# Decode attention, two blocks of 32 heads: the last quad's PV is run from the loop's own code on TensorE

## Chip, cores, metric

The kernel runs on one core of a Trainium2 chip. The metric is the device time of one execution in microseconds (us). Three executions of the kernel before took 669.31, 669.55 and 671.23 us, a median of 669.55.

## What is computed

Two independent attention blocks, A and B, each for one new token: a query projection, attention of 32 heads over a cache of 8192 keys and values of 128 elements, and an output projection. The two outputs of 512 elements are put side by side. All inputs are bf16.

```python
def _A_ref(x, k_cache, v_cache, wq, wo):          # _B_ref is the same, rep = 1
    B, Sq, D = x.shape                            # 1, 1, 512
    H, Dh = 32, 128
    q = (x @ wq).reshape(B, Sq, H, Dh).transpose(0, 2, 1, 3)
    scores = jnp.einsum("bhqd,bhkd->bhqk", q, k_cache) * (Dh ** -0.5)
    p = _softmax(scores, axis=-1)
    o = jnp.einsum("bhqk,bhkd->bhqd", p, v_cache)
    return o.transpose(0, 2, 1, 3).reshape(B, Sq, H * Dh) @ wo
```

K and V of both blocks are 268 MB, the weights 17 MB; each byte is read once.

## The kernel before

**Tiling.** The 64 heads are taken as 16 quads, `n` = 0 to 15, four heads each; quads 0 to 7 belong to A, 8 to 15 to B. A quad's K is one load of 8.4 MB: head h sits on partitions 32h to 32h + 31, and each partition holds T = 256 keys of 128 elements. K has two buffers (`kn`, slots 0 and 1, quad n in slot n % 2); V has one (`vn`).

**One quad.** DVE multiplies K by the query in place in four chunks of 64 keys (`plan_mul`, line 331). PE adds up each product over the head's elements by 16 matmuls with the identity (`plan_red`, line 340), and DVE finishes that (`plan_sr`, line 351). DVE, PE and ACT find the maximum and the exponentials `pt` (`plan_max`, `plan_gmax`, `plan_exp`). `plan_sum` (line 393) adds up the denominators on PE. `plan_pv` (line 409) is PV: 256 matmuls, one for each key column t, with `vn[:, t, :]` as weights and the four columns `pt[:, t, :]` moving, all added up in `acc`. `plan_o` (line 419) scales the result into `oD`.

**Order.** Every engine has its own list of operations, made once in Python by `op` and `wait` and written out in that order. In turn n come the three first chunks' score work of quad n, then sum and PV of quad n - 1, then the last chunk of quad n, its maximum and exponentials. SP issues all large loads: K of quad n + 1 at the start of turn n, when the reductions of quad n - 1 are done; V of quad n at the end of turn n, when PV of quad n - 1 is done. In turn 15 the output weights of A (`load_wo(0, 0)`, 4 MB) and the first two groups of B's stand in the place of the next K.

**PE's loop.** On PE alone turns 1 to 15 are a hardware loop (`_emit_loop`): the body is written once, the semaphore values waited for are kept in registers that grow from round to round, and each reduction is there twice, for the two slots of K, with a compare-and-branch that picks one. Everything before and behind the loop is straight code.

**The end.** V of quad 15 is loaded in three parts, of 128, 64 and 64 key columns (`VLAST = (0, 128, 192, 256)`). Behind them SP issues B's groups 2 to 6 of output weights. B's output weights come in groups of heads `WOG[1] = [(0, 8), (8, 4), (12, 4), (16, 8), (24, 4), (28, 2), (30, 2)]`; A's are one group. `plan_relayout(a, g)` (lines 444 to 451: DVE, PE, DVE) brings a group's outputs into the layout that `plan_wo(a, g)` (line 461) wants: four matmuls of one column for each head, 128 for A. `early` is the list of B's groups 0 to 4, whose heads belong to quads before the last; groups 5 and 6 are the last quad's. Behind the loop PE's list is (lines 525 to 543): six re-layouts, wo(0,0), wo(1,0) and wo(1,1), the sum and PV of quad 15 in three parts, wo(1,2) to wo(1,4), re-layouts 5 and 6, wo(1,5), wo(1,6), and the output.

Of the kernel before, what the change touches and what calls it, by code (L numbers as in the profile page):

```python
# [14 lines left out]
class _Ctr:  # L15


    def __init__(self, nc, stack, name):
        self.sem = stack.enter_context(nc.semaphore(name))
        self.n = 0  # L20
        self.name = name
# [29 lines left out]
def _emit(e, items, slot=None):  # L51
    for fn, ctr, k in items:
        if fn is None:
            e.wait_ge(ctr.sem, k)
        elif isinstance(fn, tuple):
            which, fns = fn
            if slot is None:
                fns[which](e).then_inc(ctr.sem, k)
            else:
                with e.If_eq(slot, 0):  # L60
                    fns[0](e).then_inc(ctr.sem, k)
                with e.Else():
                    fns[1](e).then_inc(ctr.sem, k)
        elif ctr is None:
            fn(e)
        else:
            fn(e).then_inc(ctr.sem, k)


def _steps(items):  # L70


    out, waits = [], []
    for it in items:
        if it[0] is None:
            waits.append(it[1:])
        else:
            out.append((waits, it))
            waits = []
    assert not waits  # L80
    return out


def _emit_loop(e, rounds, slot):


    rounds = [_steps(r) for r in rounds]
    assert len({len(r) for r in rounds}) == 1
    early, body = [], []
    for k in range(len(rounds[0])):  # L90
        at = [r[k] for r in rounds]
        assert all(it[1:] == at[0][1][1:] for _, it in at)
        first, second, third = at[0][0], at[1][0], at[2][0]
        waits = []
        for (ctr, v), (_, w) in zip(second, third):
            d = w - v
            assert v - d >= 1
            waits.append((ctr, v - d, d))
        for n, (ws, _) in enumerate(at[1:], 1):
            assert [(c, v) for c, v in ws] == [(c, v + n * d) for c, v, d in waits]  # L100
        for ctr, v in first:
            same = [x for c, x, _ in waits if c is ctr]
            if not same:
                early.append((None, ctr, v))
            else:
                assert v <= same[0]
        body.append((waits, at[0][1]))
    _emit(e, early)
    regs = {}
    for k, (waits, _) in enumerate(body):  # L110
        for i, (ctr, v, d) in enumerate(waits):
            if d:
                regs[k, i] = e.alloc_register("w%d_%d" % (k, i))
                e.reg_mov(regs[k, i], v)
    sreg = e.alloc_register("slot")
    e.reg_mov(sreg, slot)
    with e.Fori(0, len(rounds)):
        for k, (waits, it) in enumerate(body):
            for i, (ctr, v, d) in enumerate(waits):
                e.wait_ge(ctr.sem, regs.get((k, i), v))  # L120
            _emit(e, [it], sreg)
            for i, (ctr, v, d) in enumerate(waits):
                if d:
                    e.reg_add(regs[k, i], regs[k, i], d)
        e.reg_sub(sreg, 1, sreg)


def bass_concat_heads__mha_block_cached__gqa_block_cached__decode_kernel(
# [43 lines left out]
    with ExitStack() as st:  # L172
# [219 lines left out]
        def plan_sum(n):  # L392
            m = op("PE", lambda e: e.matmul(misc[:, 0:G], ones_f[:], rsum[:],  # L393
                                            start=True, stop=True), c_pe,
                   [p_done[n], misc_free[0]])
            r_done[n] = misc_free[0] = op("DVE", lambda e: e.reciprocal(
                rinv[:, n, :], misc[:, 0:G]), c_dve, [m])

        def plan_pv(n, t0, t1):
            for t, landed in v_in[n]:  # L400
                if t < t1:
                    wait("PE", landed)
            wait("PE", p_done[n])
            wait("PE", o_done.get(n - 1))

            def mm(e):
                r = None
                for t in range(t0, t1):
                    r = e.matmul(acc[:, 0:G], vn[:, t, :], pt[:, t, :],  # L409
                                 start=(t == 0), stop=(t == T - 1))  # L410
                return r
            if t1 == T:
                pv_done[n] = op("PE", mm, c_pv)
            else:
                op("PE", mm)

        def plan_o(n):
            a, i = divmod(n, QA)
            o_done[n] = op("DVE", lambda e: e.tensor_tensor(  # L419
                oD[:, a, G * i:G * (i + 1)], acc[:, 0:G], rinv[:, n, :], ALU.mult),  # L420
                c_dve, [pv_done[n], r_done[n]])
# [16 lines left out]
        def plan_relayout(a, g):  # L438
            h0, n = WOG[a][g]
            z = z_n[0] % 2  # L440
            z_n[0] += 1
            s = P // n
            zv = zb[:, z, :].rearrange("p (h s) -> p h s", s=s)
            m = op("DVE", lambda e: e.tensor_tensor(
                zv, oD[:, a, h0:h0 + n].unsqueeze(2).broadcast_to([P, n, s]),
                mask[n][:, None, :].broadcast_to([P, n, s]), ALU.mult),
                c_dve, [sel_ready[n], o_done[a * QA + (h0 + n) // G - 1 if (h0 + n) % G == 0 else a * QA + (h0 + n) // G], z_free.get(z)])
            z_free[z] = op("PE", lambda e: e.matmul(misc[:, 0:n], zb[:, z, :], jsel[n][:],
                                                    start=True, stop=True), c_pe, [m, misc_free[0]])
            o2_ready[a, g] = misc_free[0] = op("DVE", lambda e: e.tensor_copy(  # L450
                o2[:, a, h0:h0 + n], misc[:, 0:n]), c_dve, [z_free[z]])

        def plan_wo(a, g):

            h0, n = WOG[a][g]

            def mm(e):
                r = None
                for j in range(h0, h0 + n):
                    for i in range(NQ):  # L460
                        r = e.matmul(qyp[:, i:i + 1], wo_sb[a][:, j, i * P:(i + 1) * P],  # L461
                                     o2[:, a, j:j + 1], start=(j == 0 and i == 0),
                                     stop=(j == H - 1 and i == NQ - 1), skip_group_check=True)
                return r
            wo_done[a] = op("PE", mm, c_pe, [o2_ready[a, g], wo_in[a, g], qy_free[0]])
# [12 lines left out]


        L0, L1 = 1, NM  # L480
        marks = {}

        load_wq(0)
        load_k(0)
# [2 lines left out]
        for j in range(QA // 4):  # L487
            plan_q(0, j)
        for n in range(NM):
            marks[n] = len(pl.prog["PE"])  # L490
            if n + 1 < NM:
                load_k(n + 1)
            else:
                load_wo(0, 0)
                for g in range(BEFORE):
                    load_wo(1, g)
            plan_mul(n, 0)
            plan_red(n, 0)
            plan_mul(n, 1)
            plan_red(n, 1)  # L500
            plan_sr(n, 0)
            plan_mul(n, 2)
            plan_red(n, 2)
            plan_sr(n, 1)
            plan_mul(n, 3)
            plan_sr(n, 2)
            if n == 0:
                for j in range(QA // 4):
                    plan_q(1, j)
            else:  # L510
                plan_sum(n - 1)
                plan_pv(n - 1, 0, T)
                plan_o(n - 1)
            plan_red(n, 3)
            plan_sr(n, 3)
            plan_max(n)
            plan_gmax(n)
            plan_exp(n)
            load_v(n, VLAST if n == NM - 1 else (0, T))
        marks[NM] = len(pl.prog["PE"])  # L520
        NB = len(WOG[1])
        early = [g for g, (h0, n) in enumerate(WOG[1]) if h0 + n <= H - G]
        for g in range(BEFORE, NB):
            load_wo(1, g)
        plan_relayout(0, 0)
        for g in early:
            plan_relayout(1, g)
        plan_wo(0, 0)
        plan_y(0)
        for g in range(BEFORE):  # L530
            plan_wo(1, g)
        plan_sum(NM - 1)
        for t0, t1 in zip(VLAST, VLAST[1:]):
            plan_pv(NM - 1, t0, t1)
        plan_o(NM - 1)
        for g in early[BEFORE:]:
            plan_wo(1, g)
# [7 lines left out]
        for name, at in (("SP", block.sync), ("PE", block.tensor), ("ACT", block.scalar),  # L545
                         ("DVE", block.vector), ("POOL", block.gpsimd)):
            @at
            def _(e, name=name):
                prog = pl.prog[name]
                if name != "PE":  # L550
                    _emit(e, prog)
                    return
                _emit(e, prog[:marks[L0]])
                _emit_loop(e, [prog[marks[n]:marks[n + 1]] for n in range(L0, L1)], L0 % NK)
                _emit(e, prog[marks[L1]:])


# [26 lines left out]
```

## Time and profile before

| | |
|---|---|
| median of three runs | 669.55 us |
| profiled execution, its time | 668.77 us |
| its span, first to last instruction | 667.0 us |
| TensorE busy, matmuls / weight loads | 438.3 us (66%) / 252.4 us (38%) |
| VectorE busy | 341.3 us (51%) |
| ScalarE busy | 62.4 us (9%) |
| read from HBM | 285.21 MB, 428 GB/s over the span |
| PV matmuls, line 409 | 4096, mean 165 ns each, 109.7 us busy |
| output projection matmuls, line 461 | 256, mean 165 ns each, 7.7 us busy |
| score reductions, line 340 | 1024, mean 451 ns each, 290.6 us busy |

How to read the lines that follow: times are microseconds from the start of the span. PE is TensorE's matmuls, PEld its weight loads, DVE VectorE, ACT ScalarE, SP the engine that issues the loads (SPq its sequencer). In a line of the timeline the first number is the start, the second the duration of the piece, then engine, line of the kernel, operation, out<-in, how many of them, and in brackets how long the engine stood idle before and what ended it; "issue" means that nothing which the profile shows was waited for. A line of the chain of waits has start, duration and what the time went to. A line on a DMA queue has its kind, packets, MB and share of the 16 DMA engines' time. A line on a load has out<-in, how many, KB each and the median time from issue to landing.

### The profile page before, as it was taken

How to read it: one execution, taken by the hardware profiler on the slowest of the kernel's cores; microseconds unless marked ns; L12 is line 12 of the kernel's file. 1: busy time of each engine (PE TensorE's matmuls, PEld its weight loads, DVE VectorE, ACT ScalarE, POOL GpSimd, SP SyncE). 2: the span in 40 equal slices, each digit the busy share in tenths (PEclk: the TensorE clock that was granted, in tenths of full speed). 3: DMA queues.
4: the chain of work that ended last, by engine and by line, in shares of the span. 5: the costliest groups of instructions: out<-in, count | busy, mean ns of one | idle time of the engine just before them, and what ended most of it. 6: DMA issues, size and time to landing. Idle time of an engine off the chain costs nothing.

```text
span 667.0 us, 12144 instructions
## 1 busy us (share of the span) xinstructions
PE 438.3 (66%) x5649; PEld 252.4 (38%) x5649; DVE 341.3 (51%) x221; ACT 62.4 (9%) x151; POOL 2.8 (0%) x15
## 2 busy tenths in 40 slices
PE   2065866938387594838759483876948386694865
PEld 1022442616145261614526261442626144262555
DVE  1085908466390835638183564808365481836520
ACT  1002002020200102020100202010020202002020
POOL 1000000000000000000000000000000000000000
PEclk9999857768796676878767687877768787776775
DMA  9999999999999999999999999999999999999996
GB/s 377 438 442 437 437 434 440 428 409 436 437 436 432 440 436 441 436 421 421 436 440 428 440 436 440 436 424 421 432 440 433 432 440 440 436 440 413 408 431 285
DMA packets 6367, 285.38 MB, mean 428 GB/s; under 512 B 722, under 2 KB 724, under 8 KB 1364
## 3 DMA queue, kind: packets, MB, share of 16 engines
q1 hardware_dynamic: 6352, 285.22, 99.1%
q8 instruction: 8, 0.13, 0.1%
q14 instruction: 3, 0.02, 0.0%
q10 hardware_dynamic: 4, 0.00, 0.0%
HBM read 285.21 MB, written 0.00 MB: 428 GB/s over the span
## 4 chain that ended last, share of the span: by engine, by line
DMA 66%; PE 23%; DVE 9%; issue 1%; SPq 0%; ACT 0%
DMA kn<-in_B_k_cache_dram 21%; DMA kn<-in_A_k_cache_dram 18%; DMA vn<-in_B_v_cache_dram 18%; PE rps L340 12%; PE acc L409 10%; DMA vn<-in_A_v_cache_dram 10%; DVE kn L331 8%; DVE s_sb L351 1%; PE qyp L461 0%; PE qyp L313 0%; SPq L242 0%; ACT qbc L321 0%; PE misc L393 0%; PE bmp L472 0%; DVE out_q L475 0%
## 5 line engine op out<-in xcount | busy, mean ns | idle before, releaser
L340 PE MATMUL rps<-kn,ident 128*128 128x512 bf16 x1024 | 290.6, 451 | 170.4 <-DVE kn L331 170.4
L331 DVE TENSOR_TENSOR kn<-kn,qbc 128x8192 bf16<-128x8192 bf16 x64 | 281.4, 4418 | 97.7 <-DMA kn<-in_A_k_cache_dram 57.5
L340 PEld LDWEIGHTS rps<-kn,ident 128*128 128x128 bf16 x1024 | 111.7, 113 | 336.4 <-issue 259.9
L409 PE MATMUL acc<-pt,vn 128*128 128x4 bf16 x4096 | 109.7, 165 | 11.9 <-issue 9.1
L409 PEld LDWEIGHTS acc<-pt,vn 128*128 128x128 bf16 x4096 | 108.8, 100 | 12.9 <-issue 9.4
L351 DVE TENSOR_REDUCE s_sb<-rps 128x64 f32<-128x512 f32 x64 | 44.0, 687 | 109.1 <-PE rps L340 109.1
L388 ACT ACTIVATE pt<-s_sb,negb 32x256 bf16<-32x256 f32 x64 | 54.8, 857 | 2.1 <-ACT negb L380 0.2
L380 ACT ACTIVATE negb<-bmp 128x1 f32<-128x1 f32 x16 | 2.7, 172 | 527.1 <-PE bmp L376 527.1
L419 DVE TENSOR_TENSOR oD<-acc,rinv 128x4 bf16<-128x4 f32 x16 | 2.6, 162 | 96.1 <-PE acc L409 96.1
L376 PE MATMUL bmp<-gm,hrow 1*128 1x1 f32 x128 | 17.2, 251 | 6.0 <-DVE gm L366 6.0
L376 PEld LDWEIGHTS bmp<-gm,hrow 1*128 1x128 f32 x128 | 15.9, 191 | 10.7 <-DVE gm L366 10.0
L363 PE MATMUL mtp<-ident_f,m 128*1 128x128 f32 x32 | 6.1, 271 | 19.8 <-DVE m L357 19.8
L388 ACT ACTIVATION_READ_ACCUMULATOR pt<-s_sb,negb 32x1 f32 x64 | 15.9, 248 | 0.0
L363 PEld LDWEIGHTS mtp<-ident_f,m 128*1 128x1 f32 x32 | 1.4, 81 | 27.7 <-DVE m L357 27.7
L313 PE MATMUL qyp<-vn,xb 128*32 128x512 bf16 x64 | 6.0, 504 | 5.8 <-DMA vn<-in_A_wq_dram 4.4
L461 PE MATMUL qyp<-o,kn 128*128 128x1 bf16 x256 | 7.7, 165 | 1.8 <-issue 1.4
L366 DVE TENSOR_REDUCE gm<-mtp 1x4 f32<-1x128 f32 x16 | 4.5, 278 | 7.5 <-PE mtp L363 7.5
L461 PEld LDWEIGHTS qyp<-o,kn 128*128 128x128 bf16 x256 | 7.3, 104 | 2.0 <-issue 1.9
L393 PEld LDWEIGHTS misc<-rsum,ones_f 128*128 128x128 f32 x32 | 6.2, 198 | 2.2
L357 DVE TENSOR_REDUCE m<-s_sb 128x1 f32<-128x256 f32 x16 | 6.7, 420 | 0.5
L321 ACT CAST qbc<-qyp 128x512 bf16<-128x512 f32 x4 | 2.3, 586 | 43.9 <-PE qyp L313 43.9
L295 PE MATMUL misc<-ones_bf,kn 1*128 1x128 bf16 x4 | 0.6, 302 | 8.0 <-DMA kn<-in_B_x_dram 8.0
(31 smaller groups left out, 26.5 us busy)
## 6 DMA issues: line engine op xcount, KB each, us to landing
vn<-in_A_wq_dram SPq DMA_DIRECT2D x1, 4096.0 KB, 12.4
vn<-in_B_wq_dram SPq DMA_DIRECT2D x1, 4096.0 KB, 40.6
kn<-in_A_wo_dram SPq DMA_DIRECT2D x1, 4096.0 KB, 36.2
vn<-in_B_v_cache_dram SPq DMA_DIRECT2D x1, 4096.0 KB, 16.3
vn<-in_B_v_cache_dram SPq DMA_DIRECT2D x2, 2048.0 KB, 23.0
kn<-in_B_wo_dram SPq DMA_DIRECT2D x2, 1024.0 KB, 33.2
kn<-in_B_wo_dram SPq DMA_DIRECT2D x3, 512.0 KB, 28.8
kn<-in_B_wo_dram SPq DMA_DIRECT2D x2, 256.0 KB, 29.1
```

The lines of the kernel that those rows point to most:

```text
L313: r = e.matmul(qyp[hh * HP:(hh + 1) * HP, :].rearrange("p (i d) -> p i d", d=Dh), xb[:, a, c, hh * HP:(hh + 1) * HP], w, start=(c == 0), s ...
L331: mul_done[n, c] = op("DVE", lambda e: e.tensor_tensor(k, k, qbc[:, n:n + 1, :].broadcast_to([P, CT, Dh]), ALU.mult), c_mul, [k_in[n], qbc ...
L340: r = e.matmul(rps[:, c % 2, :].rearrange("p (t d) -> p t d", d=DW), ident[:], kn[:, i0, c * CT:(c + 1) * CT, i * DW:(i + 1) * DW], start= ...
L351: sr_done[n, c] = op("DVE", lambda e: e.tensor_reduce(s_sb[:, c * CT:(c + 1) * CT], rps[:, c % 2, :].rearrange("p (t d) -> p t d", d=DW), ...
L357: m_done[n] = op("DVE", lambda e: e.tensor_reduce(m1[:], s_sb[:], AX.X, ALU.max), c_dve, [sr_done[n, NCH - 1]])
L363: m = op("PE", lambda e: e.matmul(mtp[0:1, 0:P], m1[:], ident_f[:], start=True, stop=True), c_pe, [m_done[n], i_identf, gm_done.get(n - 1)])
L366: gm_done[n] = op("DVE", lambda e: e.tensor_reduce(gm[:], mtp[0:1, 0:P].rearrange("o (h p) -> o h p", h=G), AX.X, ALU.max), c_dve, [m, nb_ ...
L376: r = e.matmul(bmp[:, 0:1], hrow[0:1, h, :], gm[0:1, h:h + 1], start=(h == 0), stop=(h == G - 1))
L388: p_done[n] = op("ACT", lambda e, h=h, q=q: e.activation(pt[q, :, h], s_sb[q, :], AF.Exp, bias=negb[q, n:n + 1], scale=scale, accum_out=rs ...
L393: m = op("PE", lambda e: e.matmul(misc[:, 0:G], ones_f[:], rsum[:], start=True, stop=True), c_pe, [p_done[n], misc_free[0]])
L409: r = e.matmul(acc[:, 0:G], vn[:, t, :], pt[:, t, :], start=(t == 0), stop=(t == T - 1))
L461: r = e.matmul(qyp[:, i:i + 1], wo_sb[a][:, j, i * P:(i + 1) * P], o2[:, a, j:j + 1], start=(j == 0 and i == 0), stop=(j == H - 1 and i == ...
```

## The change

PE's code is arranged otherwise; the computation is the same.

- The tail's own copy of sum and PV is gone. PE's loop is put into an outer loop of two rounds. In the first the inner loop runs 15 times as before. In the second it runs once, with the score parts jumped over, so that only sum and PV are executed, now for quad 15.
- A register `left` counts from 15 down. While it isn't 0 the score parts are executed. When it is 0, PE waits for each later part of V ahead of that part. For this the loop's PV is written in the three pieces of `VLAST`.
- Between the two outer rounds PE executes the middle part: the re-layouts, wo(0,0), wo(1,0) and wo(1,1). After the second round it executes the final part from `plan_o` on. Both stand behind the inner loop under a test of `left`, the final part first.
- B's re-layouts of groups 2 to 4 move from ahead of wo(0,0) to behind wo(1,1), on DVE too, and PE waits there for the last of their copies.

The loop class keeps what `_emit_loop` did, and `emit(k, slot)` writes out step k. The diff, cut to its core:

```diff
-def _emit_loop(e, rounds, slot):
...
+class _Loop:
...
+    def emit(self, k, slot):
+        e = self.e
+        waits, it = self.body[k]
+        for i, (ctr, v, d) in enumerate(waits):
+            e.wait_ge(ctr.sem, self.regs.get((k, i), v))
+        _emit(e, [it], slot)
         for i, (ctr, v, d) in enumerate(waits):
             if d:
...
+                e.reg_add(self.regs[k, i], self.regs[k, i], d)
...
+                cuts[n].append(len(pl.prog["PE"]))
                 plan_sum(n - 1)
-                plan_pv(n - 1, 0, T)
+                for t0, t1 in zip(VLAST, VLAST[1:]):
+                    plan_pv(n - 1, t0, t1)
+                cuts[n].append(len(pl.prog["PE"]))
                 plan_o(n - 1)
...
         plan_relayout(0, 0)
-        for g in early:
+        for g in range(BEFORE):
             plan_relayout(1, g)
         plan_wo(0, 0)
         plan_y(0)
         for g in range(BEFORE):
             plan_wo(1, g)
+        for g in early[BEFORE:]:
+            plan_relayout(1, g)
+        wait("PE", misc_free[0])
+        cuts[NM].append(len(pl.prog["PE"]))
         plan_sum(NM - 1)
         for t0, t1 in zip(VLAST, VLAST[1:]):
             plan_pv(NM - 1, t0, t1)
+        cuts[NM].append(len(pl.prog["PE"]))
         plan_o(NM - 1)
...
-                _emit(e, prog[:marks[L0]])
-                _emit_loop(e, [prog[marks[n]:marks[n + 1]] for n in range(L0, L1)], L0 % NK)
-                _emit(e, prog[marks[L1]:])
+                _emit(e, prog[:cuts[L0][0]])
+                lp = _Loop(e, [prog[cuts[n][0]:cuts[n + 1][0]] for n in range(L0, L1)])
+                a, b = [len(_steps(prog[cuts[L0][0]:x])) for x in cuts[L0][1:]]
...
+                slot, left = e.alloc_register("slot"), e.alloc_register("left")
+                e.reg_mov(slot, L0 % NK)
+                e.reg_mov(left, L1 - L0)
+                with e.Fori(0, 2) as again:
+                    with e.Fori(0, (L1 - L0) - (L1 - L0 - 1) * again):
+                        with e.If_ne(left, 0):
+                            for k in range(a):
+                                lp.emit(k, slot)
+                        for k in range(a, b):
+                            if k > a + 1:
+                                with e.If_eq(left, 0):
+                                    e.wait_ge(s_v[k - a - 1].sem, 16)
+                            lp.emit(k, slot)
+                        with e.If_ne(left, 0):
+                            for k in range(b, len(lp.body)):
+                                lp.emit(k, slot)
+                            e.reg_sub(slot, 1, slot)
+                        e.reg_sub(left, left, 1)
+                    with e.If_eq(left, -1):
+                        _emit(e, prog[cuts[L1][2]:])
+                    with e.Else():
+                        _emit(e, prog[cuts[L1][0]:cuts[L1][1]])
```

## Prediction

> **What bounds the kernel now.** First the page: span, the slices of the DMA engines, the queues. The profiled execution took 668.77 us, 1.7 us more than its span; the median of the runs is 669.55, 0.8 us more.
>
> ```profile
> span 667.0 us, 12144 instructions
> ...
> DMA  9999999999999999999999999999999999999996
> ...
> q1 hardware_dynamic: 6352, 285.22, 99.1%
> ```
>
> Every slice but the last is full. 285.22 MB at the page's 428 GB/s are 666 us: inside the loop the only thing that counts is whether a load is always queued. What may differ is the end, so next the chain of waits after 632 us.
>
> ```profile
> 632.13 25.24 DMA vn<-in_B_v_cache_dram
> 657.37 0.05 issue
> 657.42 1.49 PE acc L409 x50
> 658.91 2.16 issue
> 661.07 0.51 PE acc L409 x14
> 661.58 1.71 PE qyp L461 x64
> ```
>
> The last quarter of V lands at 657.37; PE does 50 of its 64 matmuls, stands still for 2.16 us with nothing to wait for, does 14, then the output projection. Then PE alone in order of time, the first round of the loop above, a late one and the tail below:
>
> ```profile
> 84.82 3.57 PE L409 MATMUL acc<-pt,vn 128*128 128x4 bf16 x128 [0.37 <-issue]
> 92.67 1.17 PE L409 MATMUL acc<-pt,vn 128*128 128x4 bf16 x38 [4.28 <-issue]
> ...
> 624.41 6.84 PE L409 MATMUL acc<-pt,vn 128*128 128x4 bf16 x256 [0.22 <-DMA vn<-in_B_v_cache_dram]
> ...
> 648.66 0.46 PE L461 MATMUL qyp<-o,kn 128*128 128x1 bf16 x12 [1.41 <-issue]
> ...
> 654.87 2.22 PE L409 MATMUL acc<-pt,vn 128*128 128x4 bf16 x78 [2.27 <-issue]
> 657.42 1.49 PE L409 MATMUL acc<-pt,vn 128*128 128x4 bf16 x50 [0.34 <-DMA vn<-in_B_v_cache_dram]
> 661.07 0.51 PE L409 MATMUL acc<-pt,vn 128*128 128x4 bf16 x14 [2.16 <-issue]
> ```
>
> Unexplained stops come every 128 matmuls: in the tail 12 + 2 (the sum) + 114, then 78 + 50; in the loop's first round 90, 128, 38, but in a late round all 256 run in one piece. The DMA view has packets of 16 KB (0.05 MB in 3) on the queue named instruction:
>
> ```profile
> q8 instruction: 4, 0.07, 0.5%
> ...
> q8 instruction: 3, 0.05, 1.0%
> ```
>
> The first line is for 50 to 100 us, the second for 642 to 662; from 100 to 640 us there is none. So PE's code arrives in blocks of 128 matmuls with their weight loads, is stopped for when late, and the loop, whose code is loaded once, runs 15 rounds from it. In the tail stops end at 648.66, 654.87 and 661.07, one block every 6.2 us: each block is asked for when the one before is entered. That chain, not V, sets 661.07.
>
> Last, the weights of the final projection (lines 453 to 465), which SP issues from 632.61 on:
>
> ```profile
> kn<-in_B_wo_dram SPq DMA_DIRECT2D x1, 512.0 KB, 26.0
> kn<-in_B_wo_dram SPq DMA_DIRECT2D x1, 1024.0 KB, 28.1
> ...
> kn<-in_B_wo_dram SPq DMA_DIRECT2D x1, 512.0 KB, 28.8
> ...
> kn<-in_B_wo_dram SPq DMA_DIRECT2D x2, 256.0 KB, 29.1
> ```
>
> Five issues 0.47 us apart (632.61, 633.08, 633.56, 634.03, 634.50) put groups 2 to 6 in place at 658.6, 661.2, 662.4, 663.0 and 663.6. This is the second limit, just under the first.
>
> **The change, part by part.** It removes the tail's own 256 PV matmuls and their sum, two blocks of code. It adds branches, moves three re-layouts, and makes PE jump back.
>
> *Branches in the rounds.* Four compare-and-branches per round. No row times one. Below: nothing, as PE's sequencer may take them while matmuls are queued. Above: the issue piece ahead of a reduction, which holds a wait, a branch and a start: 0.14 to 0.16 us in one slot, 0.30 in the other. So 0 to 1.2 us a round. I take 0.6, and nothing on the path: in the round at 592.52 us V is issued when PV ends, while the K issued at 560.11 is there only at 605.0 (DVE starts on it at 605.04; the row's median is 45.8 us), so 12 us of transfer are queued ahead. For the last V, issued at 631.29, the cover is the 5.5 MB of output weights issued from 597.86 on, the first of which lands at 634.1 (36.2 us) and the rest by about 638: still over 2.8 us. Without cover 15 rounds would cost 9 us (0 to 18).
>
> *The middle part.* After round 15 PE jumps to the code of the 3 first re-layouts, 128 matmuls of wo(0,0), y(0), 48 of wo(1,0) and wo(1,1), and the 3 other re-layouts. SP issues nothing differently; DVE does the same 12 small operations, three pairs of them now behind the yT copy, and PE's new wait for the last copy holds only the jump back. Start 639.2 (before 638.97, plus the exit). Three re-layouts at 0.64 (starts 639.65, 640.29, 640.92) lead to 641.0. Where does code run out? The final part, 64 + 2 + 16 + 1 matmuls, lies first, the middle behind it. Counting from the block that begins at PV's 218th matmul: 38 + 32 + 10 and some waits and branches to the loop's end, about 90; 86 of the final part; so the middle begins some 48 matmuls into the block that was already loaded in the first round, and runs out after about 75 of wo(0,0), 2.1 us (3.55 for 128): 643.1. The next block was asked for at the jump, 639.2, and takes 5.4 to 7.85 us (5.4: the stop ended at 648.66 minus the block entered near the 36th matmul of wo(0,0), 643.25; 7.85: 92.67 minus 84.82; the tail has 6.2). By 6.2 it is there at 645.4. Then 53 matmuls 1.5 us, yT 0.35, 48 matmuls 1.35, three re-layouts 1.9, the last copy 0.2: **650.7** (649.9 to 652.4). The middle ends within its block, whose end lies some 20 matmuls further.
>
> *The jump back and PV.* Up to four taken branches at 0.30, 1.2 us: PV from 650.9 to 652. V's parts land at 631.29 + 16.3 = 647.6, at 652.4 and at 657.37 (the two small ones have 23.0 in the middle, the last 25.24). If the code is still there, part one takes 3.57 and part two 1.8: done by 657.4 at the latest. Part three starts at 657.42 as before, and 64 matmuls at 0.027 + 0.165 give 659.3. Before: 661.58. **PV ends 2.3 us earlier.**
>
> *What is late next.* Three branches to the final part, 0.3 to 0.9 us: 660.2. Group 2 has landed; group 3 lands at 661.2 and its 32 matmuls end at 662.1; group 4 lands at 662.4, 16 matmuls 0.45: the re-layout can start at **662.9 instead of 663.14**. From there to the end of the span the old order holds, 667.05 - 663.14 = 3.9 us, with group 6 needed at 664.0 and landed at 663.6. The stop goes, and a wait for weights takes its place: 0.24 us are left of 2.3. Code of the final part was loaded as the blocks of the loop's end and of the middle's begin: no stop.
>
> Sum: profiled 668.77 - 0.24 = 668.5; on the median 669.55 - 0.24 = **669.3**. Within its own bounds (middle up to 1.7 us later, group 4's landing give or take 0.5, chip to chip 669.31 to 671.23 in three runs) 668.3 to 670.9.
>
> **A rule against it.** The row is that the loop's end, three blocks from its head, goes back to it 14 times with no packet on the instruction queue. "Runtime: NRT & Kernel Launch", section Instruction fetch mechanics, states that a taken branch to a target outside a window of two blocks forces a fetch; by that rule each round would have fetched, which the trace excludes. The same section gives PE room for eight blocks: by it this program, about seven, would all stay, and the sum would be mine; by the window of two it would be the first rival's. No run here shows how much PE keeps beyond five blocks.
>
> **Rivals.**
>
> *The loop's code is gone when PE comes back.* For it: nothing in the trace shows that more than five blocks are held, and the middle loads one or two. Against: the five were held for 545 us. Price: from 650.7, the loop's head, then PV's first block, at 6.2 each: 663.1; then two more for PV and one for the final part, 18.6 at 6.2, or about 10.5 if a free DMA halves the delay: the last code arrives at 673.6 to 681.7 instead of 661.07, and the rest of the final part needs some 4 us more: span 678 to 686, time 680 to 688. It decides from one block on. PV takes 3.57 + 1.8 + 1.9 = 7.2 us, then 0.6 for the branches and 1.56 (663.14 - 661.58) to the re-layout, so that PV must start by 653.7 for the re-layout to be no later than 663.14; a single refetch puts the start at 650.7 + 0.6 + 6.2 = 657.5, the re-layout at 666.9, and the time at +3.7, 673.3.
>
> *The next block is asked for only when PE runs into it.* Then the middle's stop ends at 643.1 + 6.2 = 649.3, the middle at 654.6, PV starts at 655.2, and by the same sum the re-layout at 664.6: +1.4, 671.0, still within what can be told. For it: nothing; against: the steady 6.2 us from one stop to the next.
>
> *All of the 2.3 us are kept:* 667.2. For it: PE's stop is on the chain of waits; against: the landings above.
>
> *The branches show,* because the queue of loads runs dry: +9, 678. Against: 12 us of cover.
>
> **How the numbers follow.** Forecast with the asking variant 0.67; code gone altogether 0.16, one block 0.06; branches 0.03; all kept or loads sooner 0.08. About 0.3%, 2.0 us, is what a measurement of this kernel can tell from no change: faster 0.08, same 0.67, slower 0.25. The range 667.2 to 673.4 takes in the full gain and the single refetch and leaves out 0.19.
>
> **What would show it.** Right: in the PE view PV of the last round with no stop and its last part at 657.4 to 659.3; waits of L461 for kn<-in_B_wo_dram near 661 and 662.4; one or two instruction packets after 640 us instead of four; one stop in wo(0,0). Wrong: stops between 650 and 657, more packets than two there, or the last weights landing elsewhere than 663.6, which would shift everything that I computed.

## The result, and the profile after

| | before | after |
|---|---|---|
| median, 16 runs each | 669.89 us | 668.50 us |
| lowest to highest | 668.90 to 671.23 | 668.21 to 668.68 |
| profiled execution: time / span | 668.77 / 667.0 | 668.41 / 666.7 |
| ratio of the times | | 0.998, 95% interval 0.9972 to 0.9987 |

The kernel is 1.4 us faster (0.9 to 1.9 by the interval), within the 2.0 us that were named as the bound of no change, and its runs spread over 0.5 us instead of 2.3. The two profiled executions differ by only 0.36 us. Both facts need an explanation: what the change removed, and why the medians lie further apart than the profiles.

The page after, span and instruction queue:

```profile
span 666.7 us, 12274 instructions
...
q8 instruction: 6, 0.10, 0.1%
```

Six packets of code instead of eight; the two missing ones are from the tail. PE in order of time (start, duration, line, operation, tiles, count, idle time before it and what ended that):

```profile
641.79 2.14 PE L463 MATMUL qyp<-o,kn 128*128 128x1 bf16 x77
646.25 1.50 PE L463 MATMUL qyp<-o,kn 128*128 128x1 bf16 x51 [2.32 <-issue]
...
652.16 0.59 PE L395 MATMUL misc<-rsum,ones_f 128*128 128x4 f32 x2 [1.32 <-issue]
652.61 6.99 PE L411 MATMUL acc<-pt,vn 128*128 128x4 bf16 x256
659.85 0.58 PE L463 MATMUL qyp<-o,kn 128*128 128x1 bf16 x16 [0.24 <-issue]
661.08 1.01 PE L463 MATMUL qyp<-o,kn 128*128 128x1 bf16 x32 [0.66 <-DMA kn<-in_B_wo_dram]
662.34 0.59 PE L463 MATMUL qyp<-o,kn 128*128 128x1 bf16 x16 [0.24 <-DMA kn<-in_B_wo_dram]
662.79 0.17 PE L450 MATMUL misc<-jsel,zb 128*128 128x2 bf16 x1
```

There is one stop for code, in A's output projection; then PE comes back to the loop and does all 256 PV matmuls without one, ending with V's last part. PV began too late to wait for V's last part: it ran on to 659.60. The waits that remain behind it are for weights, at 661.08 and 662.34. The chain of waits (start, duration, what) now hangs on them:

```profile
634.03 28.26 DMA kn<-in_B_wo_dram
662.29 0.05 issue
662.34 0.59 PE qyp L463 x16
```

### The profile page after: what moved, and what is told of

Same layout as the page of the kernel before. It is cut to its first block, busy times and chain, and to the rows that moved or that the text cites. A ratio compares the mean times of both kernels' runs of the same rounds, so it can differ in the third digit from the quotient of the medians.

```text
span 666.7 us, 12274 instructions
## 1 busy us (share of the span) xinstructions
PE 441.5 (66%) x5649; PEld 252.7 (38%) x5649; DVE 341.5 (51%) x221; ACT 62.4 (9%) x151; POOL 2.8 (0%) x15
## 4 chain that ended last, share of the span: by engine, by line
DMA 62%; PE 25%; DVE 10%; issue 1%; another core or an unknown queue 0%; SPq 0%; ACT 0%
DMA kn<-in_B_k_cache_dram 21%; DMA kn<-in_A_k_cache_dram 19%; PE rps L342 15%; DMA vn<-in_A_v_cache_dram 14%; PE acc L411 10%; DVE kn L333 9%; DMA vn<-in_B_v_cache_dram 5%; DMA kn<-in_B_wo_dram 4%; DVE s_sb L353 1%; SPq L244 0%; PE qyp L315 0%; PE qyp L463 0%; PE misc L395 0%; ACT qbc L323 0%
## 5 line engine op out<-in xcount | busy, mean ns | idle before, releaser
L342 PE MATMUL rps<-kn,ident 128*128 128x512 bf16 x1024 | 294.6, 456 | 171.7 <-DVE kn L333 171.7
L378 PEld LDWEIGHTS bmp<-gm,hrow 1*128 1x128 f32 x128 | 15.6, 187 | 10.7 <-DVE gm L368 10.0
L390 ACT ACTIVATION_READ_ACCUMULATOR pt<-s_sb,negb 32x1 f32 x64 | 15.9, 248 | 0.0
```

What stands on the lines that cost most here:

```text
L342: r = e.matmul(rps[:, c % 2, :].rearrange("p (t d) -> p t d", d=DW), ident[:], kn[:, i0, c * CT:(c + 1) * CT, i * DW:(i + 1) * DW], start= ...
L378: r = e.matmul(bmp[:, 0:1], hrow[0:1, h, :], gm[0:1, h:h + 1], start=(h == 0), stop=(h == G - 1))
L390: p_done[n] = op("ACT", lambda e, h=h, q=q: e.activation(pt[q, :, h], s_sb[q, :], AF.Exp, bias=negb[q, n:n + 1], scale=scale, accum_out=rs ...
```

## The experiments

**Theory 1:** before the change, the end is set by blocks of PE code loaded one after the other, and since that chain begins and runs differently in each execution, so does the end. The change takes this chain out of the way, and the weights' landings, which hardly vary, are left. **Theory 2:** the spread and the gain come from something else, transfers or the loop's rounds.

### Second profile of the kernel before

No edit.

> The kernel before, unchanged, for a second profile of it. Theory 1 (code loads in series set its end, and each load's delay differs from run to run): the last weights land within 0.3 us of 663.6 again, but the last stop in PV ends at a time other than 661.07, between 661 and 664, and the span follows that stop one for one. Theory 2 (the code loads are steady, and what spreads the runs of before over 2.3 us is the transfers): stops at 648.7, 654.9 and 661.1 give or take 0.3, and the weights land later in a slower run.

669.67 us median of 12 runs, 668.67 to 671.16; ratio 0.9997 (0.9987 to 1.0008). Its profiled execution was again one of the quickest, 668.79 us, with the stops ending at 648.68, 654.88 and 661.08, as in the first profile. Those are the stops that theory 2 named, but in an execution of the same time theory 1 has them there too. It says how much the runs differ and not yet why.

### Third and fourth profile

> Before, unchanged, for a profile of one of its slower executions. Where the time lies over 669.5, theory 1 has it in the chain of code loads alone: the last weights within 0.4 us of 663.6, a stop in PV's last part that ends after 661.5, and the span longer by as much. Theory 2 (transfers): the weights later by as much as the span.

> As for the third: another profile of the kernel before. Theory 1: the end of the last stop and the span move together from profile to profile, while the weights' last landing stays within 0.4 us of 663.6. Theory 2: the weights move with the span.

670.68 and 669.53 us, one execution each. The third execution's chain of waits:

```profile
654.50 2.27 issue
656.77 3.55 PE acc L409 x128
660.32 2.65 issue
662.97 0.51 PE acc L409 x14
663.48 1.71 PE qyp L461 x64
```

All of it is PE and its code; V's last part, there at 657.3, is not on the chain any more. The profiles side by side (the first re-layout on PE is where the loop is left; the weights are SP's last issue plus its 29.0 us or so):

| execution, time | loop left | last stop ends | last weights | span |
|---|---|---|---|---|
| first, 668.77 | 638.97 | 661.07 | 663.6 | 667.0 |
| fourth, 669.53 | 640.29 | 661.82 | 663.5 | 667.8 |
| third, 670.68 | 640.69 | 662.97 | 663.6 | 669.0 |
| after, 668.41 | 640.43 | none in PV | 663.6 | 666.7 |

The stop's end and the span move together, 1.9 and 2.0 us from the first to the third, and the weights stand still: theory 1. The fourth profile lies between them; its last stop, and the re-layout that follows in the fourth and in the third:

```profile
661.82 0.51 PE L409 MATMUL acc<-pt,vn 128*128 128x4 bf16 x14 [2.37 <-issue]
...
663.90 0.17 PE L448 MATMUL misc<-jsel,zb 128*128 128x2 bf16 x1
```

```profile
665.05 0.17 PE L448 MATMUL misc<-jsel,zb 128*128 128x2 bf16 x1
```

Why the third left its loop later shows in the windows of 631 to 639 us (PE, PEld, DVE, ACT, POOL busy, then PE's granted clock, DMA share, GB/s), first execution and third:

```profile
631.00:639.00 8.00, 6.39 (x37) 2.99 (x34) 1.75 (x5) 0.00 (x0) 0.00 (x0) 0.83 0.99 418
```

```profile
631.00:639.00 8.00, 6.76 (x27) 2.34 (x24) 1.27 (x3) 0.00 (x0) 0.00 (x0) 0.66 1.02 430
```

The granted clock was 0.83 in the one and 0.66 in the other, and the loop's last 16 reductions took 4.88 and 6.28 us. The run after left its loop nearly as late as the third one of before, at a clock of 0.71, and still ended earliest. It looks most like the fourth, which lost its time earlier, in the reductions from 606 to 616 us. First execution, fourth, and after:

```profile
606.00:616.00 10.00, 6.22 (x21) 2.49 (x22) 8.68 (x4) 0.00 (x0) 0.00 (x0) 0.64 0.97 419
```

```profile
606.00:616.00 10.00, 6.32 (x17) 2.36 (x18) 7.71 (x2) 0.00 (x0) 0.00 (x0) 0.53 0.97 419
```

```profile
606.00:616.00 10.00, 6.31 (x17) 2.29 (x18) 7.72 (x2) 0.00 (x0) 0.00 (x0) 0.54 0.98 426
```

The slowest execution profiled took 670.68 us; what one above 671 looks like is not shown.

### One block less of code in the tail

```diff
-        for t0, t1 in zip(VLAST, VLAST[1:]):
+        for t0, t1 in zip(VLAST[1:], VLAST[2:]):
             plan_pv(NM - 1, t0, t1)
```

(and `start` is set on the first matmul that is left)

> Before, without the first 128 of the tail's 256 PV matmuls: the last quad's output lacks V's first part, all loads stay. The tail's code is one block shorter, with no second round and no branch. Theory 1 (code loads in series set the end of before and its spread): no stop in PV's last part, PV ends at 659.3, the output projection waits for weights at 661.1 and 662.4, the re-layout is at 662.8 give or take 0.2, median 668.5, highest below 669.2, ratio 0.998. Theory 2 (the spread comes from the turns of the loop or from the transfers, which the change alters by its branches): median 669.9, runs up to 671 as before.

668.48 us, 668.13 to 669.03, ratio 0.9979 (0.997 to 0.9988): the time after the change without its second round. PE:

```profile
658.00 1.87 PE L409 MATMUL acc<-pt,vn 128*128 128x4 bf16 x64 [3.00 <-DMA vn<-in_B_v_cache_dram]
659.73 0.56 PE L462 MATMUL qyp<-o,kn 128*128 128x1 bf16 x16
661.75 1.01 PE L462 MATMUL qyp<-o,kn 128*128 128x1 bf16 x32 [1.45 <-DMA kn<-in_B_wo_dram]
```

V's last part runs in one piece, and what is waited for is weights. In this profiled execution, its slowest at 669.03, all landings were some 0.5 us later than elsewhere, the re-layout with them (663.41). This kernel, which leaves out the first part of quad 15's PV, drops 128 matmuls and their code; the change keeps the matmuls and drops the code alone, and both come to 668.5 us. So it is the code that cost.

### The moved re-layouts alone

```diff
-        for g in early:
+        for g in range(BEFORE):
             plan_relayout(1, g)
...
             plan_wo(1, g)
+        for g in early[BEFORE:]:
+            plan_relayout(1, g)
         plan_sum(NM - 1)
```

> Before, with the three re-layouts moved behind wo(1,1) as in the change, and nothing else. Theory 1: the block in which wo(0,0) lies is left 1.9 us earlier or nearly so, the chain of four loads starts at about 641.4 instead of 643.25, the last stop ends near 659.3, PV's last 14 matmuls end at 659.8, and weights decide: the re-layout at 662.9, the median 668.5 to 669.0. Theory 2: 669.9, as before.

670.14 us, ratio 1.0006 (0.9996 to 1.0015): no gain, against the expectation. From the loop's exit at 639.91 to the last stop's end it still took 22.3 us (22.1 in the first profile of before):

```profile
647.81 0.38 PE L461 MATMUL qyp<-o,kn 128*128 128x1 bf16 x9 [1.52 <-issue]
...
656.00 3.57 PE L409 MATMUL acc<-pt,vn 128*128 128x4 bf16 x128 [2.54 <-issue]
...
662.20 0.53 PE L409 MATMUL acc<-pt,vn 128*128 128x4 bf16 x14 [2.63 <-issue]
```

A block asked for at 647.8 was there only at 656.0, 8.2 us later, where the others took 6.2. PE reached that border 1.8 us earlier, counted from the loop's exit (7.9 us behind it instead of 9.7), and the block was there no earlier (16.1 us behind it instead of 15.9). Why it took longer is not shown; that it meets other loads is a guess. The move is not what made the gain.

### The change without the move

```diff
         plan_relayout(0, 0)
-        for g in range(BEFORE):
+        for g in early:
             plan_relayout(1, g)
...
-        for g in early[BEFORE:]:
-            plan_relayout(1, g)
         wait("PE", misc_free[0])
```

> After, with the three re-layouts back ahead of wo(0,0). Theory 1: the time after is set by weights, so 668.5 again; the stop in wo(0,0) shrinks from 2.3 to about 0.4 us, since the block is still asked for at the jump, and PV starts near 651.0 instead of 652.6. If the move were what made the gain: 669.9.

668.48 us, 668.27 to 668.69, ratio 0.9978 (0.997 to 0.9987): as after. A's projection runs in one piece, 3.82 us, and PV starts at 649.0 instead of 652.6, which nothing waits for. I had expected 651.0 and a stop of 0.4 us; there is none.

### Spare code ahead of the loop

```diff
+        def spare(e):
+            r = None
+            for _ in range(56):
+                r = e.matmul(bmp[:, 256:260], ident[:], ones_bf[:, 0:4], start=True, stop=True)
+            return r
+        wait("PE", i_ident)
+        op("PE", spare)
         for n in range(NM):
```

> Before, with 56 spare matmuls on PE ahead of the loop, so that the loop's end reaches into the next block of code and the tail's first block is loaded in the first round. No branch, no second round. Theory 1 (loads in series): the stop at 648.7 goes, the chain is one block shorter, the last block is there by about 658, PV ends at 659.3 to 660, the re-layout starts near 662.9 after a wait for weights; three instruction packets after 640 us instead of four; time as after the change, 668.5, a ratio of 0.998. Theory 2 (something else of the change made the gain, such as the loop's second round or its split PV): ratio 1.000, with the median at 669.9.

669.46 us, 668.95 to 669.92, ratio 0.9991 (0.9983 to 1.0). The expectation was wrong: the tail's first block was not loaded in the first round. There are five packets after 640 us, not three, and the stops merely fall elsewhere, the last one, 1.02 us, into B's projection:

```profile
658.51 2.00 PE L409 MATMUL acc<-pt,vn 128*128 128x4 bf16 x69 [2.63 <-issue]
...
663.61 0.29 PE L461 MATMUL qyp<-o,kn 128*128 128x1 bf16 x5 [1.02 <-issue]
```

The first stop comes 243 matmuls behind the loop, 13 short of two blocks, so by this count the loop's end reached some 13 matmuls into a new block. Entering a block by so little did not make PE load the next one in 15 rounds; what does was not tried further. The time, between the two that were expected (668.5 and 669.9), decides nothing.

### Without the last weights, after and before

```diff
-        for g in range(BEFORE, NB):
-            load_wo(1, g)
...
-                        r = e.matmul(qyp[:, i:i + 1], wo_sb[a][:, j, i * P:(i + 1) * P],
+                        w = j % 4 if g >= BEFORE else j
+                        r = e.matmul(qyp[:, i:i + 1], wo_sb[a][:, w, i * P:(i + 1) * P],
```

(and no wait for those loads)

> After, without the loads of B's output weights of groups 2 to 6 (2.5 MB): their projections use group 0's weights. If, as I hold, those landings set the end after the change, nothing is waited for between PV's end at 659.4 and the re-layout, which comes at 661.5 instead of 662.8: 1.2 to 1.4 us less, median 667.2. If the end is set by PE's own work after V: 668.5 as after.

> Before, without the same loads. Theory 1: code sets the end here, so the last stop still ends near 661, or up to 1 us earlier because the block asked for at 654.9 meets no loads after 657.4; median 669.0 to 669.9, and the runs still spread over more than 1 us. If weights set the end of before too: about 668.5.

After: 667.42 us, 666.86 to 667.98, ratio to before 0.9965 (0.9953 to 0.9977). The 64 matmuls run in one piece, the re-layout is at 661.35 instead of 662.79: the weights were the limit.

```profile
659.62 1.86 PE L464 MATMUL qyp<-o,kn 128*128 128x1 bf16 x64 [0.24 <-issue]
```

Before: 667.38 us, 666.28 to 668.72, ratio 0.997 (0.996 to 0.9979), a much larger fall than I expected under theory 1 (669.0 to 669.9). Its profiled execution, the quickest of the twelve, shows no stop in V's last part:

```profile
654.65 2.22 PE L409 MATMUL acc<-pt,vn 128*128 128x4 bf16 x78 [2.00 <-issue]
657.22 1.87 PE L409 MATMUL acc<-pt,vn 128*128 128x4 bf16 x64 [0.34 <-DMA vn<-in_B_v_cache_dram]
```

The block asked for at 654.65 came with a packet between 655.5 and 657; with the weights' loads behind V, the one asked for at 654.87 had none before 658.5. The instruction queue from 655.5 to 657 us, without those loads:

```profile
q8 instruction: 1, 0.02, 3.9%
```

So this block's delay came from the loads queued beside it, and taking loads away took the chain's last stop away too, in this execution. This pair shows the limit of the kernel after; it doesn't separate the theories for the kernel before, and its runs still spread over 2.4 us.

### More code between the loop and its second round

```diff
+        def spare(e):
+            r = None
+            for _ in range(128):
+                r = e.matmul(bmp[:, 256:260], ident[:], ones_bf[:, 0:4], start=True, stop=True)
+            return r
+        wait("PE", nb_done[NM - 1])
+        op("PE", spare)
         wait("PE", misc_free[0])
```

(256 matmuls in the second kernel)

> After, with 128 spare matmuls on PE at the end of the middle part, one more block of code between the loop and its second round. If PE keeps eight blocks: three instruction packets after 640 us (two in the run after), a stop of about 0.8 us in the spare matmuls, PV from 656.5 without a stop, the re-layout at 665.6, 2.8 us more than after: 671.3. If it keeps only seven or fewer, the loop's head is gone when PE comes back: stops of 3.5 to 6.2 us at the jump back and in PV, five to eight packets, 680 or more.

> After, with 256 spare matmuls there, two more blocks. If PE keeps eight blocks, the ninth in a row takes the place of the one with the loop's head: four packets for the new blocks and then one for each block of the loop, eight to ten after 640 us, a stop at the jump back and two in PV, 3.5 us each with the loads over: 688 to 694. If it keeps nine or more: four packets, PV without a stop, 677.4. This prices the rival of a refetch, which the change escapes.

One block more, 671.34 us in its one execution, about the 671.3 that eight kept blocks gave. Packets of code after 636 us, then PE:

```profile
q8 instruction: 3, 0.05, 0.4%
```

```profile
652.89 2.88 PE L544 MATMUL bmp<-ones_bf,ident 128*128 128x4 bf16 x102 [1.21 <-issue]
656.25 0.59 PE L395 MATMUL misc<-rsum,ones_f 128*128 128x4 f32 x2 [0.48 <-issue]
656.70 6.99 PE L411 MATMUL acc<-pt,vn 128*128 128x4 bf16 x256
```

Two more, 685.94 us in its one execution, the same two views:

```profile
q8 instruction: 10, 0.16, 1.3%
```

```profile
668.62 0.59 PE L395 MATMUL misc<-rsum,ones_f 128*128 128x4 f32 x2 [8.41 <-issue]
669.07 2.49 PE L411 MATMUL acc<-pt,vn 128*128 128x4 bf16 x88
671.91 3.53 PE L411 MATMUL acc<-pt,vn 128*128 128x4 bf16 x125 [0.36 <-issue]
675.96 1.28 PE L411 MATMUL acc<-pt,vn 128*128 128x4 bf16 x43 [0.52 <-issue]
```

With the first, PV is whole. With the second the loop's head is gone: 8.41 us at the jump back, then a stop at each block's border, and every block of the loop is loaded anew. Count the five blocks that the prediction has PE hold through the loop, and the packets behind it: two for the change make seven, three with one spare block make eight, and the two spare blocks make nine. By that count PE keeps eight and gives up the oldest. The sum for the second was 2 us too high at its lower end: with the loads over, a block comes in some 4 us (675.96 minus 671.91), nearly as fast as PE works through one, and the stops in PV are 0.4 to 0.5 us instead of 3.5.

### The change with the last two re-layouts early

```diff
-        for g in early[BEFORE:]:
-            plan_wo(1, g)
+        plan_wo(1, BEFORE)
         for g in range(len(early), NB):
             plan_relayout(1, g)
-        for g in range(len(early), NB):
+        for g in range(BEFORE + 1, NB):
             plan_wo(1, g)
```

(on top of the change without the move)

> After, with the three early re-layouts back ahead of wo(0,0) and the last quad's two re-layouts taken ahead of wo(1,3). They then lie in the wait for weights at 661.0, and behind group 6's landing at 663.5 only 8 matmuls, the yT copy and the output are left: the yT copy at 664.0 instead of 664.26, 0.2 to 0.4 us less than after, median 668.2. If the wait for group 4 is not what decides, 668.5.

668.31 us, 668.12 to 668.48, ratio to before 0.9979 (0.9971 to 0.9988). The re-layouts lie in the wait for weights, and all that is left behind the last landing is one group:

```profile
660.88 0.19 PE L450 MATMUL misc<-jsel,zb 128*128 128x2 bf16 x1 [0.46 <-DVE zb L446]
...
663.81 0.35 PE L463 MATMUL qyp<-o,kn 128*128 128x1 bf16 x8 [0.34 <-DMA kn<-in_B_wo_dram]
```

It is the lowest median of a kernel that computes all, 0.2 us below the change; the two were not timed side by side, and so small a step is not shown by these runs.

## Why the prediction was right, and where it was not

**What bounds the end.** Right: blocks of code in series. A block less in the tail gives the whole gain; the move of the re-layouts gives none of it, and the change does as well without it. PV ended 2.0 us earlier than in the first profile (659.60 instead of 661.58), not 2.3, for it began too late to wait for V's last part; 0.66 us of waiting for weights behind it hid that.

**Branches.** Nothing on the path, as taken. Three of them between PV and the projection cost 0.24 us (0.3 to 0.9 was allowed), the sum began 1.12 us after the last copy, with the jump back between them (1.2 at most), and V was issued at 631.76 instead of 631.29 without a gap in the transfers.

**The middle part.** The stop in wo(0,0) came after 77 matmuls (about 75 predicted) and ended 5.8 us after the loop's exit at 640.43. The sum ahead of PV began at 652.16 and PV at 652.61, just past the late end of 650.9 to 652, because the loop was left 1.2 us later than the 639.2 that I started from. The fourth execution of before, left at 640.29 with no new branch in it, shows that this is PE's clock: 0.53 from 606 to 616 us there and 0.54 after, 0.64 in the first profile. The branches added some 0.15 us at the exit, the idle time ahead of the first re-layout.

**What is late next.** Right, to 0.12 us: weights at 661.08 and 662.34 (661.2 and 662.4 predicted), the re-layout at 662.79 (662.9), the span 666.7 (666.8).

**The rule.** With one spare block the loop's code was still whole, with two it was not: by the count above, PE keeps eight blocks. The Trainium skill, "Runtime: NRT & Kernel Launch", section Instruction fetch mechanics, gives PE room for as many, and these runs agree. The window of two in the same section doesn't hold for PE here.

**The rivals.** The refetch exists, and it decides two blocks further on than this program goes: 685.9 us, between the 680 and 688 given for it, though with two spare blocks in it. That it falls there is luck: the two blocks alone were to take 677.4, so the refetch cost some 8.5 us by my estimate, where the prediction had at least 10.7 (680 less 669.3). Asking only when PE runs into a block: no, the middle's block was there 2.3 us after PE ran into it, and none has come in less than some 5.1 while the loads flowed. The branches never showed.

**The step that was mis-sized** is the carrying over: "on the median 669.55 - 0.24 = 669.3". The 0.24 us is the difference to one execution of before, the first profile. The term in it is the re-layout at 663.14: it is 663.90 and 665.05 in the fourth and third profile, while the re-layout after stands on the weights, whose last landing was within 0.3 us of 663.6 in every profile but that of the shortened tail. I took 6.2 us a block and an exit at 638.97 for steady; the first profile was in fact near the fastest execution of before, and it lay 0.8 us under the median that was shown, which the prediction notes in its first paragraph and then doesn't use. The gain on the median is 1.4 us instead of 0.24; the sign, the mechanism and the new limit hold, and 668.5 was inside the forecast's own 668.3 to 670.9.

## What to carry to other kernels

Straight code of some hundred matmuls at the end of a kernel is loaded block by block while the last data still flow, and stops with nothing to wait for at equal counts of matmuls, 128 here, are its mark. Code that a loop has already brought in was run again here with no packet and no stop, as long as the blocks from its head to the jump, with the one loaded ahead, were no more than eight. Where the end hangs on such a chain, one profile is one draw of it: compare its time with the median, and with the spread, before a saving in microseconds is carried over. And price the next limit first: of the 2.3 us that the stops cost in the first profile, the weights' landings left 0.35 (the re-layout at 662.79 instead of 663.14).

## What was unexpected of the hardware

- A block of code (128 matmuls with their weight loads, 16 KB) takes from 5.1 to 8.2 us from one border to the next while loads flow and about 4 us when they are over; asked for 1.8 us earlier, one came no earlier.
- A block that PE entered by about 13 matmuls, by count, in each of 15 rounds did not make it load the next one.
- PE's granted clock in the loop's last turn was 0.83 in one execution and 0.66 in another of the same kernel, 1.4 us on 16 matmuls of 512 columns. Before the change, loops left 1.32 and 1.72 us later ended 0.8 and 2.0 us later; after it, runs whose loops were left at 639.44 (without the move) and at 640.43 ended within 0.2 us of each other.
